# Attention and two expert layers on one core: an earlier load, a split moved to another engine, two small steps put later

## The chip, the cores and the metric

The kernel runs on one core of a Trainium2 chip. A core has a matrix engine (PE, with its weight loads shown as PEld), a vector engine (DVE), a scalar engine (ACT), a general engine (POOL), and a sync engine (SP) whose queue issues all DMA transfers of this kernel. The engines run beside each other, each one through its own instructions in a fixed order, and wait for each other by semaphores. The metric is the device time of one execution in microseconds (us); lower is better.

## What is computed

```
q, k, v: (2, 8, 576, 64)        1152 tokens, d_model 512
scores  = q @ k.T / 8
mask    = heads 0-3: 0 <= pos_q - pos_k < 32
          heads 4-7: pos_k <= pos_q and pos_q % 32 == pos_k % 32
x       = softmax(masked scores) @ v              -> (1152, 512)
p       = domain_probs / sum(domain_probs)        -> (1152, 4)
x2      = sum_e p[:, e] * (relu(x @ w1[e]) @ w2[e])    w1: (4, 512, 1024)
out     = (sigmoid(x2 @ wg) * (x2 @ wv)) @ wo          wg, wv: (512, 1536)
```

## The kernel before

**Attention.** Its 32 groups of scores (16 a batch: eight "strided" ones for heads 4 to 7, eight "local" ones for heads 0 to 3) pass through a pipeline that is written out by hand. At step i, `attention()` emits the scores and the exponentials of group i, the normalisation (`group_norm`) of group i-2, the transpose (`group_transpose`) of group i-4, the product with v of group i-5 and the copy into the token matrix (`group_split`) of group i-6. The first 23 steps (`FIRST_GROUPS`) run alone; the others are emitted between the first matmuls of the expert layer. `keep_warm` adds two matmuls with zeros to some steps.

In a step, DVE copies a transpose out of PSUM (L524), takes row maxima (L503), adds a small number to the row sums (L512) and inverts them (L513); POOL multiplies the probabilities by them (L514); for some steps DVE then rounds the result to its high part (L567, L561) and POOL subtracts to get the low part `xl` (L568, L562). ACT makes the exponentials (L505).

**Loads of q and k for the strided heads.** `load_strided_qk(b, c)` loads heads 4+2c and 5+2c of batch b, one DMA for q and one for k when b is 1, into a corner of the accumulator `x2acc` that is not in use yet (72 partitions x 2 x 512 floats, 295 KB each). `qk_strided` transposes them on PE (L445), in steps 13 and 15 for pair (1, 0) and in steps 17 and 18 for pair (1, 1). All loads stand in SP's queue in the order in which the program asks for them.

**Weights.** They come in 25 pieces of 512 x 512, in two raw loads each of 512 KB for the first 16, through three raw buffers. Pieces 0 to 3 are split into a high part (ACT, L425) and a low part (DVE, L427), both float32r, four chunks of 512 columns each. From step 14 on, `prep_some(0, 1)` does one such step behind each attention step, so that piece 0's four low parts follow steps 15, 17, 19 and 21. Pieces 4 to 15 are made half precision by `prep_half`: DVE takes maxima of both raw loads (L339) and of these (L344), PE spreads the maximum to all partitions (L251, in `scale_on_chip`), DVE makes a scale of it (L254 to L258), and ACT and DVE write the parts (L353, L355). `yield "hold"` ends the budget of the current tile; a tile is twelve matmuls (four triples L612, L613, L614), and each tile's end gives `prep_some` two or three steps.

**Token weights.** `token_weights()` is four small DVE operations (L194 to L197), `spread_token_weights()` a PE transpose (L201), a copy and two DMAs, which bring the first expert's weights to all partitions.

Of the kernel before, what the change touches and what calls it, by code (L numbers as in the profile page):

```python
# [9 lines left out]
F32 = mybir.dt.float32  # L10
# [7 lines left out]
ALU = mybir.AluOpType  # L18
# [15 lines left out]
FIRST_GROUPS = 23  # L34
# [4 lines left out]
def attn_moe_glu_kernel(ctx, tc, q, k, v, dp, w1, w2, wg, wv, wo, out):  # L39
    nc = tc.nc  # L40
# [206 lines left out]
    def scale_on_chip(col, m):  # L247

        ps = g_tile()
        top = m.bitcast(BF16)[:, 1:2]  # L250
        nc.tensor.matmul(ps[:, :128], top.to_broadcast([128, 128]), identb, start=True, stop=True)  # L251
        t = tmp["top"][:, n_top[0] % 2:n_top[0] % 2 + 1]
        n_top[0] += 1
        nc.vector.tensor_reduce(t, ps[:, :128], AX.X, ALU.max)  # L254
        nc.vector.tensor_scalar(t.bitcast(U32), t.bitcast(U32), 0x7F800000, None, ALU.bitwise_and)
        dn = tmp["down"][:, col:col + 1]
        nc.vector.tensor_scalar(dn, t, 2.0 ** -100, 1.0 / TOP, ALU.max, ALU.mult)
        nc.vector.reciprocal(tmp["up"][:, col:col + 1], dn)  # L258
        yield "hold"
# [69 lines left out]
    def w_pool(name):  # L329
        return tmp["w"] if name == "w2" else wp  # L330

    def prep_half(n):

        i, u, m = raw_list[n]
        r = held_raw[i, u] = raw.pop((i, u))
        if u == 0:
            held_raw[i] = tmp["p"].tile([128, 3], F32, tag="wpk", name="wpk")
        pk = held_raw[i]
        nc.vector.tensor_reduce(  # L339
            pk[:, u // 2:u // 2 + 1], r, AX.XY, ALU.max, apply_absolute_value=True)  # L340
        yield
        if u == 0:
            return
        nc.vector.tensor_reduce(pk[:, 2:3], pk[:, :2], AX.X, ALU.max)  # L344
        yield "hold"
        yield from scale_on_chip(i, pk[:, 2:3])
        (name, tag), = pool_of[i]
        t = w_pool(name).tile([128, 2, 4, 512], F16, tag=tag, name="w16")
        wh[i], wl[i] = t[:, 0], t[:, 1]
        sc = tmp["up"][:, i:i + 1]  # L350
        for c in range(4):
            part = held_raw[i, c // 2 * 2][:, c % 2, :]
            nc.scalar.activation(wh[i][:, c, :], part, AF.Copy, scale=sc)  # L353
            yield
            nc.vector.scalar_tensor_tensor(wl[i][:, c, :], part, sc, wh[i][:, c, :], ALU.mult, ALU.subtract)  # L355
            yield
            if c == 1:
                held_raw.pop((i, 0))
                load_raw_to(n + RAW_BUFS)
        for k_ in ((i, 2), i):  # L360
            held_raw.pop(k_)
        load_raw_to(n + 1 + RAW_BUFS)
# [48 lines left out]
    def prep_weights(n):  # L411
        i, u, m = raw_list[n]
        if i >= 2 * NST:
            yield from prep_gated(n)
            return
        if as_half(i // 2):
            yield from prep_half(n)
            return
        if u == 0:
            for d, (name, tag) in zip((wh, wl), pool_of[i]):  # L420
                d[i] = w_pool(name).tile([128, 4, 512], F32R, tag=tag, name=tag)
        r = raw.pop((i, u))
        hi_, lo_ = wh[i][:, u:u + m, :], wl[i][:, u:u + m, :]
        for x in range(m):
            nc.scalar.copy(hi_[:, x], r[:, x])  # L425
            yield
            nc.vector.tensor_tensor(lo_[:, x], r[:, x], hi_[:, x].bitcast(F32), ALU.subtract)  # L427
            yield
        load_raw_to(n + 1 + RAW_BUFS)

# [4 lines left out]
    def qk_strided(b, c, hhs):  # L435

        for hh in hhs:
            for nm, dst in (("qs", QT), ("ks", KT)):
                if hh == 0:
                    dst["s", b, c] = atp.tile([128, 2, 4, NU], F32, tag=nm + "T", name=nm + "T", bufs=2)  # L440
                src, t = qkv[nm, b, c], dst["s", b, c]
                ps = gp.tile([128, 512], F32, tag="g", name="qkps")
                pv_ = ps[:, :4 * NU].rearrange("p (a b) -> p a b", b=NU)
                for rp in range(4):
                    nc.tensor.transpose(  # L445
                        pv_[:, rp, :], src[:, hh, rp * 128:(rp + 1) * 128], ident[:NU, :NU]
                    )
                if nm == "qs":
                    nc.scalar.activation(t[:, hh], pv_, AF.Copy, scale=SCALE)
                else:  # L450
                    nc.vector.tensor_copy(t[:, hh], pv_)
        if hhs[-1] == 0:
            return
        if (b, c) == (0, 1):
            alloc_x(NT - 1)
        if (b, c) == (1, 0):
            load_strided_qk(1, 1)

    def qk_local(b, part):
        for nm, dst in (("ql", QT), ("kl", KT)):  # L460
# [142 lines left out]
    def g_tile():  # L603
        n_g[0] += 1
        pool = tmp["g"] if "g" in tmp and n_g[0] % 8 >= PSUM_BUFS else gp
        return pool.tile([128, 512], F32, tag="g", name="gps")
# [206 lines left out]
    with tc.manual_schedule():  # L813
        acc["x2"] = accp.tile([128, KC, NTOK], F32, tag="acc", name="x2acc")
        load_strided_qk(0, 0)
        load_strided_qk(0, 1)
        warm_up()
        make_constants()
        load_local(0)
        load_strided_v(0, 0)  # L820
        load_strided_v(0, 1)
        load_vl(0)
        nc.sync.dma_start(ptok, dp.rearrange("(t p) e -> p t e", p=128))
        for T in range(NT - 1):
            alloc_x(T)

        def attend():

            i = next(att, None)
            if i == 1:  # L830
                load_strided_qk(1, 0)
                load_raw_to(3)
            if i == 8:
                load_strided_v(1, 0)
            if i == 11:
                load_local(1)
            if i == 13:
                load_strided_v(1, 1)
            if i == 18:
                token_weights()  # L840
            if i == 19:
                spread_token_weights()
            if i == 20:
                load_vl(1)
            return i

        att = attention()
        for i in range(FIRST_GROUPS):
            attend()
            if i >= 14:  # L850
                prep_some(0, 1)
        n_none = 0
        halves = x_half()
        for n, u in enumerate(units):
            if u == ("u", EARLY, 0):
                for _ in halves:
                    pass
            if u[0] == "u" and u[1] == NST:
                while u[2] not in x2_done:
                    split_x2(1)  # L860
            if n == N_EARLY:
                while attend() is not None:
                    pass
                at_stack.close()
                tmp["p"] = ctx.enter_context(tc.tile_pool(name="tmp", bufs=2, side="right", reuse_waits="tile"))
                alloc_scales()
                late.append(raw_next[0])
                tmp["g"] = ctx.enter_context(
                    tc.tile_pool(name="gp2", bufs=8 - PSUM_BUFS, space=PSUM, side="right", reuse_waits="tile"))
                tmp["w"] = ctx.enter_context(tc.tile_pool(name="wp2", bufs=W_BUFS_2, side="right", reuse_waits="tile"))  # L870
            while any(i in pieces_of(u) for i in waiting()):
                prep_some(n, 1)
            if u == ("d", NST, 0):
                acc["out"] = accp.tile([128, NTB, DM], F32, tag="acc", name="outacc")
            if n >= N_EARLY:
                load_p_some(n)
                load_p_some(n)
            for y in unit_steps(u):
                if n < N_EARLY and y is None:
                    n_none += ATT_RATE  # L880
                    while n_none >= 1:
                        attend()
                        n_none -= 1
                if y == "evac":
                    if n >= N_EARLY:

                        if gated:
                            split_x2(2)
                            continue
                        if x16_next[0] < 2 or n > units.index(("u", EARLY - 1, x16_next[0] - 1)):  # L890
                            if next(halves, "end") != "end":
                                prep_some(n, 1)
                                continue
                    prep_some(n, 3 if u[1] >= NST else 2)
            if u[0] == "d" and u[1] == NST - 1:
                gated.append(x2_half(u[2]))
# [28 lines left out]
```

## Time and profile before

| | |
|---|---|
| median of 3 runs | 677.48 us (676.19 to 678.43) |
| profiled execution | 675.37 us, span 673.6 us |
| PE busy | 658.9 us, 98% of the span |
| DVE, ACT, POOL busy | 489.5, 269.0, 196.5 us |
| granted PE clock, mean | 0.992 of full speed |

The span is the profiled stretch from the first to the last instruction; 1.8 us of the execution's time lie around it. The profiled execution is 2.1 us below the median of the timed runs.

### The profile page before, as it was taken

How to read it: one execution, taken by the hardware profiler on the slowest of the kernel's cores; microseconds unless marked ns; L12 is line 12 of the kernel's file. 1: busy time of each engine (PE TensorE's matmuls, PEld its weight loads, DVE VectorE, ACT ScalarE, POOL GpSimd, SP SyncE). 2: the span in 40 equal slices, each digit the busy share in tenths (PEclk: the TensorE clock that was granted, in tenths of full speed). 3: DMA queues.
4: the chain of work that ended last, by engine and by line, in shares of the span. 5: the costliest groups of instructions: out<-in, count | busy, mean ns of one | idle time of the engine just before them, and what ended most of it. 6: DMA issues, size and time to landing. Idle time of an engine off the chain costs nothing.

```text
span 673.6 us, 11048 instructions
## 1 busy us (share of the span) xinstructions
PE 658.9 (98%) x4263; PEld 430.6 (64%) x4263; DVE 489.5 (73%) x986; ACT 269.0 (40%) x665; POOL 196.5 (29%) x218
## 2 busy tenths in 40 slices
PE   9979999999899999999999999999999999999998
PEld 5657899999766666666665656556655555555554
DVE  4866765888777777779798989887789898822212
ACT  6757631333344434442425252533355264331120
POOL 3634540000222222222345252522144244331110
PEclk9969999999999999999999999999999999999999
DMA  8944133011322342233221313111123321000002
GB/s 191 227 111 122 49 112 89 27 37 32 106 75 64 93 106 75 75 94 95 63 79 59 95 32 94 53 43 33 31 63 94 95 85 40 1 1 0 32 17 94
DMA packets 39029, 48.59 MB, mean 72 GB/s; under 512 B 18524, under 2 KB 23424, under 8 KB 38976
## 3 DMA queue, kind: packets, MB, share of 16 engines
q1 hardware_dynamic: 38976, 47.89, 25.0%
q8 instruction: 33, 0.54, 0.3%
q14 instruction: 20, 0.16, 0.1%
HBM read 45.50 MB, written 2.38 MB: 71 GB/s over the span
## 4 chain that ended last, share of the span: by engine, by line
PE 89%; DVE 8%; issue 1%; DMA 1%; ACT 1%; POOL 0%; SPq 0%; POOLq 0%; DVEq 0%; ACTq 0%
PE gps L612 27%; PE gps L613 27%; PE gps L614 27%; PE sps L495 2%; PE tps L521 1%; PE o L542 1%; PE warm L167 1%; DMA x2acc<-in_q_dram 1%; PE qkps L445 1%; DVE x2acc L676 1%; DVE wpk L339 1%; PE sps L485 1%; ACT P L505 1%; DVE x L290 1%; DVE magn L372 1%
## 5 line engine op out<-in xcount | busy, mean ns | idle before, releaser
L635 POOL TENSOR_TENSOR hl<-t,hh 128x384 f16<-128x384 f32 x72 | 69.3, 962 | 253.9 <-ACT t L634 249.8
L612 PEld LDWEIGHTS <-w 128*128 128x128 f16 x864 | 84.4, 98 | 56.2 <-issue 0.3
L614 PEld LDWEIGHTS <-w 128*128 128x128 f16 x864 | 84.4, 98 | 56.0
L613 PEld LDWEIGHTS <-w 128*128 128x128 f16 x864 | 84.4, 98 | 55.2
L633 ACT ACTIVATE hh<-gps 128x384 f16<-128x384 f32 x72 | 35.2, 489 | 148.3 <-PE gps L614 147.2
L612 PE MATMUL gps<-x,w 128*128 128x384 f16 x288 | 93.9, 326 | 0.0
L612 PE MATMUL gps<-hh,w 128*128 128x384 f16 x288 | 93.9, 326 | 0.0
L614 PE MATMUL gps<-x2p,w 128*128 128x384 f16 x288 | 93.9, 326 | 0.0
L614 PE MATMUL gps<-hh,w 128*128 128x384 f16 x288 | 93.9, 326 | 0.0
L613 PE MATMUL gps<-hl,w 128*128 128x384 f16 x288 | 93.9, 326 | 0.0
L613 PE MATMUL gps<-x,w 128*128 128x384 f16 x288 | 93.9, 326 | 0.0
L614 PE MATMUL gps<-x,w 128*128 128x384 f16 x288 | 93.9, 326 | 0.0
L613 PE MATMUL gps<-x2p,w 128*128 128x384 f16 x288 | 93.9, 326 | 0.0
L612 PE MATMUL gps<-x2p,w 128*128 128x384 f16 x288 | 93.9, 326 | 0.0
L699 POOL TENSOR_TENSOR hl<-gv,hh 128x384 f16<-128x384 f32 x36 | 34.7, 965 | 146.4 <-ACT hh L698 146.4
L355 DVE SCALAR_TENSOR_TENSOR w<-raw,up,w 128x512 f16<-128x512 f32 x48 | 38.4, 799 | 20.3 <-ACT w L353 20.3
L676 DVE TENSOR_TENSOR x2acc<-x2acc,t 128x384 f32<-128x384 f32 x84 | 49.7, 591 | 2.9
L673 DVE SCALAR_TENSOR_TENSOR t<-gps,comb,pb 128x384 f32<-128x384 f32 x72 | 43.9, 609 | 9.9 <-PE gps L614 9.9
L698 ACT CAST hh<-gv 128x384 f16<-128x384 f32 x36 | 18.4, 512 | 81.4 <-DVE gv L697 81.4
L697 DVE SCALAR_TENSOR_TENSOR gv<-gps,sg 128x384 f32<-128x384 f32 x36 | 20.0, 555 | 40.5 <-PE gps L614 40.3
L407 POOL TENSOR_TENSOR w<-magn,w 128x512 f16<-128x512 f32 x36 | 46.1, 1287 | 8.5 <-ACT magn L406 8.0
L353 ACT ACTIVATE w<-raw,up 128x512 f16<-128x512 f32 x48 | 33.0, 717 | 31.4 <-DVE up L258 31.0
(130 smaller groups left out, 1238.5 us busy)
## 6 DMA issues: line engine op xcount, KB each, us to landing
raw<-in_moe_w_dram SPq DMA_DIRECT2D x32, 512.0 KB
raw<-in_moe_w_gate_dram SPq DMA_DIRECT2D x12, 512.0 KB
raw<-in_moe_w_val_dram SPq DMA_DIRECT2D x12, 512.0 KB
raw<-in_moe_w_out_dram SPq DMA_DIRECT2D x12, 512.0 KB
pb<-pd SPq DMA_DIRECT2D x11, 192.0 KB
out_dram<-outacc SPq DMA_DIRECT2D x8, 256.0 KB
vl<-in_v_dram SPq DMA_DIRECT2D x8, 160.0 KB
vs<-in_v_dram SPq DMA_DIRECT2D x4, 288.0 KB
```

Of the source, the lines that this page charges most:

```text
L353: nc.scalar.activation(wh[i][:, c, :], part, AF.Copy, scale=sc)
L355: nc.vector.scalar_tensor_tensor(wl[i][:, c, :], part, sc, wh[i][:, c, :], ALU.mult, ALU.subtract)
L407: nc.gpsimd.tensor_tensor(wl[i][:, c, :], f, wh[i][:, c, :], ALU.subtract)
L612: nc.tensor.matmul(ps, ah, bh, start=i == 0, stop=False)
L613: nc.tensor.matmul(ps, ah, bl, start=False, stop=False)
L614: nc.tensor.matmul(ps, al, bh, start=False, stop=i == n - 1)
L633: nc.scalar.activation(dh, ps, AF.Relu, scale=DOWN)
L635: nc.gpsimd.tensor_tensor(dl, t, dh, ALU.subtract)
L673: nc.vector.scalar_tensor_tensor(t, ps, cc, pb[e, T], ALU.mult, ALU.mult)
L676: nc.vector.tensor_tensor(a, a, t, ALU.add)
L697: nc.vector.scalar_tensor_tensor(gv, pv_, DOWN, sg, ALU.mult, ALU.mult)
L699: nc.gpsimd.tensor_tensor(dl, gv, dh, ALU.subtract)
```

## The change

The load of pair (1, 1) is asked for behind step 1, next to pair (1, 0) and three raw loads, instead of at the end of step 15. Piece 0's four low parts are subtracted on POOL. The token weights are made and spread behind steps 23 and 24 instead of 18 and 19. In `prep_half` there is a second "hold" between the maximum of a piece and the matmul that spreads it.

```diff
@@ prep_half
         nc.vector.tensor_reduce(pk[:, 2:3], pk[:, :2], AX.X, ALU.max)
+        yield "hold"
         yield "hold"
         yield from scale_on_chip(i, pk[:, 2:3])
@@ prep_weights
             nc.scalar.copy(hi_[:, x], r[:, x])
             yield
-            nc.vector.tensor_tensor(lo_[:, x], r[:, x], hi_[:, x].bitcast(F32), ALU.subtract)
+            low = nc.gpsimd if i == 0 else nc.vector
+            low.tensor_tensor(lo_[:, x], r[:, x], hi_[:, x].bitcast(F32), ALU.subtract)
             yield
@@ qk_strided
-        if (b, c) == (1, 0):
-            load_strided_qk(1, 1)
@@ attend
             if i == 1:
                 load_strided_qk(1, 0)
                 load_raw_to(3)
+                load_strided_qk(1, 1)
...
-            if i == 18:
+            if i == FIRST_GROUPS:
                 token_weights()
-            if i == 19:
+            if i == FIRST_GROUPS + 1:
                 spread_token_weights()
```

On SP's queue, between steps 1 and 20, the order differs as follows (x2acc with q and k is the pair of the strided heads, vs and vl are v, ql and kl the local heads' q and k, raw the weights, pd and ptokT the token weights):

```order
 L143 DMA raw<-in_moe_w_dram 128x2x512 x3
+L82 DMA x2acc<-in_q_dram 72x2x512
+L82 DMA x2acc<-in_k_dram 72x2x512
 L90 DMA vs<-in_v_dram 72x2x512
 L101 DMA ql<-in_q_dram 128x9x64 x2
 L101 DMA kl<-in_k_dram 128x9x64 x2
 L90 DMA vs<-in_v_dram 72x2x512
-L82 DMA x2acc<-in_q_dram 72x2x512
-L82 DMA x2acc<-in_k_dram 72x2x512
```

The pair has moved ahead of both loads of vs and of the local heads' four loads.

On POOL, in steps 14 to 19 (P is the normalisation, xl the low part of a result, wl<-raw,wh the low part of a weight chunk):

```order
-L514 TENSOR_TENSOR P<-P,sm 96x384 x2
+L514 TENSOR_TENSOR P<-P,sm 96x384
+L429 TENSOR_TENSOR wl<-raw,wh 128x512
+L514 TENSOR_TENSOR P<-P,sm 96x384
 L568 TENSOR_TENSOR xl_167<-of,xh_166 128x288
 L514 TENSOR_TENSOR P<-P,sm 96x384
+L429 TENSOR_TENSOR wl<-raw,wh 128x512
 L514 TENSOR_TENSOR P<-P,sm 72x288
 L568 TENSOR_TENSOR xl_167<-of,xh_166 128x288
```

A subtraction of 512 columns now stands between two normalisations in every second step.

On DVE, where piece 6 is prepared (wpk its maxima, top the start of its scale), the rows were, in the kernel before:

```order
L339 TENSOR_REDUCE wpk<-raw 128x1
L675 TENSOR_TENSOR t<-gps,pb 128x384
L676 TENSOR_TENSOR x2acc<-x2acc,t 128x384
L339 TENSOR_REDUCE wpk<-raw 128x1
L344 TENSOR_REDUCE wpk<-wpk 128x1
L254 TENSOR_REDUCE top<-gps 128x1
```

and are, in the changed kernel:

```order
L676 TENSOR_TENSOR x2acc<-x2acc,t 128x384
L356 SCALAR_TENSOR_TENSOR w_2124<-raw,up,w_2124 128x512
L339 TENSOR_REDUCE wpk<-raw 128x1 x2
L344 TENSOR_REDUCE wpk<-wpk 128x1
L254 TENSOR_REDUCE top<-gps 128x1
L255 TENSOR_SCALAR top<-top 128x1
```

On PE, the matmul L251 that lies between L344 and L254 stood behind the first tile of its unit before, and stands behind the third now: 24 matmuls further down.

## Rows read from the trace of the kernel before

**Rows 1.** Page, part 1: busy us, share of the span, instructions.
```profile
PE 658.9 (98%) x4263; PEld 430.6 (64%) x4263; DVE 489.5 (73%) x986; ACT 269.0 (40%) x665; POOL 196.5 (29%) x218
```
**Rows 2.** PE's waits: us in total, times, longest.
```profile
PE qkps L445 <- DMA x2acc<-in_q_dram: 4.1, 1, 4.1
PE gps L251 <- DVE wpk L344: 2.0, 2, 1.7
...
PE gps L251 <- DVE gpk L396: 0.7, 1, 0.7
```
**Rows 3.** Windows around the longest wait: length, busy by engine, PEclk, DMA, GB/s.
```profile
36.40:38.40 2.00, 0.00 (x0) 0.00 (x0) 1.24 (x5) 2.00 (x12) 1.86 (x3) 0.95 0.79 205
38.40:40.50 2.10, 0.01 (x1) 0.04 (x1) 0.00 (x0) 1.10 (x8) 0.50 (x1) 0.50 0.65 158
40.50:48.50 8.00, 7.84 (x58) 5.82 (x59) 4.98 (x17) 3.21 (x15) 1.48 (x3) 0.50 0.21 66
```
**Rows 4.** Timeline of SP's queue: start, us to issue.
```profile
20.16 1.41 SPq L143 DMA_DIRECT2D raw<-in_moe_w_dram  x3
...
33.06 1.45 SPq L90 DMA_DIRECT2D vs<-in_v_dram  x1
34.55 0.45 SPq L82 DMA_DIRECT2D x2acc<-in_q_dram  x1
```
**Rows 5.** Chain of waits, the same stretch: start, us, what.
```profile
34.55 5.80 DMA x2acc<-in_q_dram
```
**Rows 6.** Windows ahead of the wait, columns as in rows 3.
```profile
20.00:28.00 8.00, 7.25 (x107) 5.09 (x103) 6.44 (x22) 5.65 (x29) 5.06 (x8) 1.00 0.95 281
28.00:32.00 4.00, 4.00 (x53) 3.12 (x49) 3.77 (x15) 3.11 (x15) 2.68 (x4) 1.00 1.08 166
```
**Rows 7.** Timeline of PE where the expert layer begins.
```profile
55.81 0.45 PE L613 MATMUL gps<-xl,wh 128*128 128x384 f32 x1 [0.53 <-POOL xl L568]
```
**Rows 8.** Subtractions on DVE and POOL: ns min/median/max; then by form, 26 to 57 us.
```profile
L427 DVE TENSOR_TENSOR wl<-raw,wh x16: 656/685/1276, 34.1 to 97.1; 128x512 fp32r<-128x512 f32 x16
...
L407 POOL TENSOR_TENSOR w<-magn,w x36: 1156/1304/1607, 333.1 to 592.4; 128x512 f16<-128x512 f32 x36
...
L568 POOL TENSOR_TENSOR xl<-of,xh 128x288 fp32r<-128x288 f32 x2 | 1.6, 790 | 0.0
...
L568 POOL TENSOR_TENSOR xl<-of,xh 128x96 fp32r<-128x96 f32 x2 | 0.8, 384 | 0.0
```
**Rows 9.** Timeline of DVE: small operations from SBUF to SBUF.
```profile
33.02 0.59 DVE L512 TENSOR_SCALAR sm<-sm 96x3 f32<-96x3 f32 x1
...
36.02 0.15 DVE L512 TENSOR_SCALAR sm<-sm 96x3 f32<-96x3 f32 x1
...
45.92 0.60 DVE L195 TENSOR_SCALAR psums<-psums 128x9 f32<-128x9 f32 x1
```
**Rows 10.** Timeline of POOL.
```profile
32.90 1.09 POOL L562 TENSOR_TENSOR xl<-of,xh 128x192 fp32r<-128x192 f32 x2
...
36.54 0.82 POOL L514 TENSOR_TENSOR P<-P,sm 96x384 f32<-96x384 f32 x1 [1.73 <-DVE sm L513]
...
45.70 0.79 POOL L568 TENSOR_TENSOR xl<-of,xh 128x288 fp32r<-128x288 f32 x1
...
54.75 0.66 POOL L514 TENSOR_TENSOR P<-P,sm 72x288 f32<-72x288 f32 x1 [1.74 <-DVE xh L567]
55.38 0.94 POOL L568 TENSOR_TENSOR xl<-of,xh 128x96 fp32r<-128x96 f32 x2
```
**Rows 11.** Timeline of DVE where piece 6's maximum is taken.
```profile
169.87 1.21 DVE L339 TENSOR_REDUCE wpk<-raw 128x1 f32<-128x1024 f32 x1
171.11 0.15 DVE L344 TENSOR_REDUCE wpk<-wpk 128x1 f32<-128x2 f32 x1
```
**Rows 12.** Timeline of PE, the last 24 matmuls ahead of the L251 that reads it.
```profile
165.51 0.34 PE L612 MATMUL gps<-x,w 128*128 128x384 f16 x1
...
169.26 0.33 PE L614 MATMUL gps<-x,w 128*128 128x384 f16 x1
```

## The prediction

> **What bounds the kernel now.** I read the page first: PE is busy for 658.9 of 673.6 us [rows 1], so no other engine's work counts unless PE waits for it or runs slower because of it. Next PE's own waits. Three matter: 4.1 us once for the DMA that brings q of a strided pair, 2.0 us in two waits for a weight piece's maximum (one of them 1.7), and 0.7 us for a later piece's [rows 2]. Then the windows around the long wait, where the reader is to see two losses, not one. PE does nothing from 36.4 to 40.5; from 38.4 on the granted clock is 0.50, that is 1.2 GHz, and it is still 0.50 in the eight microseconds after the wait, in which PE is busy for 7.84 [rows 3]. At 2.4 GHz that work takes about half, 3.9 us. So the late load costs up to 4.1 + 3.9 = 8.0 us.
>
> Why it is late: SP is in order, and it got to this load only at 34.55, behind a load of v that held it from 33.06 to 34.5 [rows 4]. From there it took 5.80 us to land, because the DMA engines were still busy with what was asked for earlier [rows 5, 6].
>
> Last, the place where attention hands over to the expert layer: PE's first matmul that needs the last low part `xl` of token block 0 starts at 55.81, after a wait for POOL [rows 7]. Whatever the change does in steps 14 to 22 shows as a shift of this one time; behind it PE is fed well enough that I carry the shift to the end.
>
> **The load, part by part.** In the new order the pair stands behind pair (1, 0) and three raw loads. These are 2 x 0.295 + 3 x 0.524 = 2.16 MB; the window from 20 to 28 us moved 281 GB/s x 8 us = 2.25 MB [rows 6], so the raws are in by about 28. The pair's 0.59 MB at the next window's 166 GB/s [rows 6] take 3.6 us: landed by 31.6. PE asks for it at 36.4 [rows 3]; the cover is nearly 5 us. The wait goes (gain 4.1) and with it the reason for the slow clock. Pair (1, 0) and the raws stand ahead of it and lose nothing. What is now behind it, two loads of v and the local q and k, lands up to 3.6 us later, but the same bytes are through by the same time as before, 34.55 + 5.80 = 40.35. The first of them to be used is local q and k, in step 21, which I put at about 44 below; if this cover went, PE would wait there instead.
>
> **What is late next.** Without the wait PE alone would come to the handover some 9 us earlier: 4.1 for the wait, 3.9 for the clock, and about 1.2 of small waits at 53 to 56. It won't, because POOL's row gets full. POOL's normalisation at 36.54 had 1.73 us of idle time before it [rows 10], into which the first low part fits. From there to the `xl` that PE needs, POOL now has: two normalisations of 384 columns (2 x 0.82), five of 288 (5 x 0.66), two `xl` of 288 columns (2 x 0.79), one split pair (0.94), the first of the last pair (0.38), and three low parts [rows 8, 10]. A low part on POOL is not in the trace. The nearest row is the subtraction of 512 columns with half-precision output, 1.16 to 1.61 us with a median of 1.30 [rows 8]; the same operation at 96 and 288 columns, 0.384 and 0.790, gives 2.1 ns a column and 1.26 us at 512. I take 1.29. The sum is 1.64 + 3.30 + 1.58 + 0.94 + 0.38 + 3.87 = 11.7, so POOL is done at 48.2 if it never waits. That makes 7.6 us instead of 9.
>
> It will wait. The operation L512 of DVE takes 0.15 us by itself but 0.59 at 33.02, where it began beside a POOL operation of 32.90 and ended with it; L195 did the same at 45.92, beside the POOL subtraction that began at 45.70 [rows 9, 10]. So a small DVE operation stands still until POOL's current one is through, and the next normalisation needs just this L512. Behind each of the three low parts, POOL then idles while DVE finishes L512, the reciprocal and a rounding: from L512's start at 36.02 to POOL's at 36.54 that is 0.5 us [rows 9, 10]. With a fourth, shorter one of 0.3 that is 1.8 us, and the handover is at 50.0: 5.8 us earlier. At two of the places DVE and POOL come within 0.1 us of each other by my count, and either could be first. I take 6.2 us, near the lower end of 5.8 to 7.6.
>
> The page "SBUF — State Buffer" of the Trainium skill, section "Who interferes with whom", says that such pairs hold a shared port as an exclusive lock, and that whoever comes first blocks the other for the whole instruction. By that rule the 5.8 stands and the 7.6 doesn't. The two long rows agree with it.
>
> What DVE is spared is the four low parts: 0.69 us each at the median, up to 1.28 beside POOL [rows 8]. I price this at nothing beyond the above, since POOL sets the pace there.
>
> **Token weights.** Four small DVE operations, the longest 0.60 us [rows 9], a short PE transpose, a copy and two DMAs go from steps 18 and 19 into the expert layer's first unit. PE pays for the transpose in either place. Their result is used by the first down unit, at least 14 triples later (42 matmuls at 0.163 = 6.8 us, worked out in the next part); the DMAs lie on a queue that is mostly idle by then (share 0.21 in rows 3). I price this at 0; if the two took as long as the late load, PE would wait up to 2 x 5.8 - 6.8 = 4.8 us. On SP the raw loads behind them move by as much, with two other raws in hand.
>
> **The second hold.** DVE is late for piece 6: its second maximum runs from 169.87 and L344 ends at 171.26, while PE was through at about 169.6 [rows 11, 12]. PE's matmul L251 now stands 24 matmuls further down. These take (169.26 - 165.51) / 23 = 0.163 us each [rows 12], 3.9 us together, against a wait of 1.7; DVE has one more L355 to do in between, under 0.8. So this wait goes, and the shorter one of piece 4, a tile further down, too: 2.0 us [rows 2]. The bounds are 0 and 2.0; nothing speaks for a part of it. Each of twelve pieces starts its scale a tile later, and the half-ready pieces of the last layer follow; counted in the program's order, pieces 20 and 23 are now written 6 tiles ahead of their first use instead of 13, 12 x 0.163 x 6 = 11.7 us. The 0.7 us of [rows 2] may come, go or double: plus or minus 0.7.
>
> **Sum.** 6.2 + 2.0 = 8.2. The profiled execution's 675.4 becomes 667.2. The median of the runs is 2.1 above it, so the prediction is 677.5 - 8.2 = 669.3.
>
> **The rivals.**
> *The clock falls again at the handover* (671 to 674). In the count above PE has its last work before the handover at about 48 and waits for `xl` until 50: 2 us, and before, the clock fell some 2.0 us after PE went idle [rows 3]. A second stretch of 10 us at 1.2 GHz, now under dense matmuls, costs 5 us: 674. Against it: if DVE wins either tie the gap is nearer 1 us.
> *POOL is worse than counted* (671 to 673). With low parts at 1.61 [rows 8] POOL needs 3 x 0.32 = 1.0 us more, and with an idle half microsecond in each of eight steps 2.2 more than the 1.8 taken: a gain of 6.2 - 3.2 + 2.0 = 5.0, 672.5. "GPSIMD Engine Reference" of the Trainium skill, section 3.1, speaks against this part of the change: it counts 2.6 cycles an element for a two-input operation there and keeps elementwise work on DVE; 512 elements at 1.2 GHz would be 1.11 us by its figure, an estimate. The rows agree on the ratio (1.30 against 0.69), and the outcome of the rule is this rival.
> *The wait only moves* (675 to 677.5). Local q and k land after step 21 asks for them. The wait and the slow clock of [rows 3] come back there, 8.0 us against the 6.2; what is left is the hold's 2.0. Against it: 40.35 is before 44 with 3.6 us to spare.
> *Slower* (above 679.5). The pieces that are now 6 tiles ahead are not in time: DVE would have to be 11.7 us behind in the last layer, and each microsecond beyond that is a microsecond of PE at pieces 20 and 23. It decides from 11.7 + 8.2 + 2 = 22 us on, 11 if both are late alike after the cover. Against it: nine L251 of that layer had one tile of cover, 2.0 us, and PE waited 0.7 in all [rows 2], so DVE was under 3 us behind.
>
> **Chances and range.** The forecast, 666 to 671: 0.65. Clock: 0.13. POOL: 0.12. The wait moved: 0.06. Slower: 0.03. Another 0.01 lies below. The likeliest is 669.3. The range goes down to 665.8 (7.6 for the handover, 2.0, and the 0.7 of the gpk waits, with about 1.4 from waits behind the handover that I didn't count) and up to 673.5, which takes in the POOL rival and most of the clock's. 0.3% of this kernel is 2.0 us, about what the measurement can tell from no change. Faster by more: 0.92; within: 0.05; slower: 0.03.
>
> **What would show it.** PE's wait for x2acc is gone, and the PEclk is 1.00 from 36 to 50: right on the load. PE's waits name POOL (L514, L568, L429) between 40 and 50 instead, and the first L613 that reads `xl` starts at 49.6, give or take 1: right on the next bound. The POOL rows of the low parts are 1.2 to 1.4 us, and L512 has rows of 0.5 us and more beside them. No wait of PE for L344. Wrong would be: a window with 0.50 behind the handover, PE waiting for ql or kl, or for a weight in the last layer.

## Result and the profile after

The changed kernel takes 669.87 us (median of 4 runs, 669.53 to 670.36) against 676.84 us (675.8 to 678.43, 4 runs) for the kernel before in the same comparison: a ratio of 0.9896, 95% interval 0.9873 to 0.9918. The profiled execution has a span of 668.3 us instead of 673.6. Two executions further down, of 845.45 us (u_load) and 1746.33 us (hold_some, its first profiled one), are out of line with all others and stand in no median or ratio.

The page of the changed kernel, part 1, and the line of the granted clock in 40 slices (9 is 90% or more of full speed; the third slice, which holds the wait, was a 6 before):

```profile
PE 655.2 (98%) x4258; PEld 429.0 (64%) x4263; DVE 483.3 (72%) x982; ACT 267.9 (40%) x665; POOL 200.4 (30%) x222
...
PEclk9999999999999999999999999999999999999999
```

PE's waits in the changed kernel, in the columns of [rows 2]:

```profile
PE gps L251 <- DVE gpk L397: 3.4, 2, 1.7
PE tps L521 <- POOL P L514: 2.0, 5, 0.9
...
PE gps L613 <- POOL xl L568: 0.6, 1, 0.6
```

The wait for x2acc and the waits for the half-precision pieces (wpk) are gone, 6.1 us together. POOL's normalisations stand in the first one's place with 2.0 us, as the prediction had it. The top row has grown: 3.4 us for two pieces of the last layer, where it was 0.7 for one.

The same stretches as in [rows 3], and the one up to the handover:

```profile
36.40:38.40 2.00, 1.06 (x13) 0.92 (x12) 1.93 (x8) 1.79 (x9) 1.60 (x3) 1.00 1.06 232
38.40:40.50 2.10, 2.10 (x39) 1.70 (x37) 1.65 (x4) 1.72 (x11) 2.10 (x3) 1.00 0.83 188
40.50:48.50 8.00, 6.96 (x84) 5.11 (x82) 7.34 (x22) 7.42 (x41) 6.79 (x10) 1.00 0.62 149
48.50:50.10 1.60, 0.81 (x5) 0.24 (x3) 1.06 (x5) 1.60 (x8) 1.20 (x4) 1.00 0.53 116
```

The clock is 1.00 where it was 0.50, and DVE, ACT and POOL are all nearly full: where one transfer held the stretch up, three engines are now near their limit in it.

SP's queue of the changed kernel, as in [rows 4]:

```profile
21.41 0.48 SPq L82 DMA_DIRECT2D x2acc<-in_q_dram  x1
21.93 0.39 SPq L82 DMA_DIRECT2D x2acc<-in_k_dram  x1
...
30.20 6.34 SPq L101 DMA_DIRECT2D kl<-in_k_dram  x2
36.63 1.01 SPq L90 DMA_DIRECT2D vs<-in_v_dram  x1
```

The load is asked for 13.1 us earlier. The second load of v is now last, 3.6 us later than before, and nothing waits for it.

The handover on PE, as in [rows 7], then POOL and DVE where the second low part stands (their timelines):

```profile
50.09 0.44 PE L613 MATMUL gps<-xl,wh 128*128 128x384 f32 x1 [0.64 <-POOL xl L568]
```

```profile
39.42 1.28 POOL L429 TENSOR_TENSOR wl<-raw,wh 128x512 fp32r<-128x512 f32 x1
41.10 0.66 POOL L514 TENSOR_TENSOR P<-P,sm 72x288 f32<-72x288 f32 x1 [0.40 <-PE tps L521]
```

```profile
39.77 0.95 DVE L512 TENSOR_SCALAR sm<-sm 72x4 f32<-72x4 f32 x1
40.76 0.17 DVE L513 RECIPROCAL sm<-sm 72x4 f32<-72x4 f32 x1
```

Read the three together: L512 begins 0.35 us after POOL's subtraction and ends when that one does (40.70); the reciprocal and a rounding follow; POOL starts its next normalisation 0.40 us after it became free. The profile puts this wait of POOL down to a transpose. But POOL has five such gaps from 36 to 50 us, put down to four different operations, and in all five it starts 0.17 or 0.18 us after the reciprocal's end; so what it waits for is DVE. Without POOL beside it L512 would have been done at about 39.9 (0.15 us alone), well before POOL was free.

### The profile page after: what moved, and what is told of

It is laid out like the page before. It is cut to its first block, busy times and chain, and to the rows that moved or that the text cites. A ratio compares the mean times of both kernels' runs of the same rounds, so it can differ in the third digit from the quotient of the medians.

```text
span 668.3 us, 11027 instructions
## 1 busy us (share of the span) xinstructions
PE 655.2 (98%) x4258; PEld 429.0 (64%) x4263; DVE 483.3 (72%) x982; ACT 267.9 (40%) x665; POOL 200.4 (30%) x222
## 4 chain that ended last, share of the span: by engine, by line
PE 85%; DVE 10%; ACT 2%; issue 1%; POOL 1%; ACTq 0%; POOLq 0%; DVEq 0%
PE gps L612 26%; PE gps L613 26%; PE gps L614 26%; PE sps L495 2%; PE tps L521 2%; DVE bits L377 1%; DVE magn L380 1%; PE warm L167 1%; PE o L542 1%; DVE bits L375 1%; DVE x2acc L676 1%; DVE bits L371 1%; DVE outacc L725 1%; DVE gpk L393 1%; ACT magn L407 1%
## 5 line engine op out<-in xcount | busy, mean ns | idle before, releaser
L676 DVE TENSOR_TENSOR x2acc<-x2acc,t 128x384 f32<-128x384 f32 x84 | 51.8, 617 | 2.9
L408 POOL TENSOR_TENSOR w<-magn,w 128x512 f16<-128x512 f32 x36 | 44.4, 1232 | 25.6 <-ACT magn L407 24.7
L254 DVE TENSOR_REDUCE top<-gps 128x1 f32<-128x128 f32 x27 | 7.9, 291 | 51.4 <-PE gps L251 51.3
L505 ACT ACTIVATE P<-sps,nm 72x72 f32<-72x72 f32 (+1 forms) x112 | 36.4, 334 | 16.5 <-DVE sm L512 12.4
```

Source lines behind the costliest of these rows:

```text
L408: nc.gpsimd.tensor_tensor(wl[i][:, c, :], f, wh[i][:, c, :], ALU.subtract)
L505: nc.scalar.activation(pp[:, j, :], pv_[:, j, :], AF.Exp, bias=nm[:n, j:j + 1], accum_out=sm[:n, j:j + 1])
L676: nc.vector.tensor_tensor(a, a, t, ALU.add)
```

## Experiments

Each kernel is the changed one or the one before with the edit shown. "Handover" is the start of the first matmul that reads the last `xl` (55.81 before, 50.09 after), from the profile of each; ratios are to the kernel before, timed beside each group, with 95% intervals. An edit shifts the line numbers behind it: the reciprocal is L513 in the changed kernel and L512 in no_add, the normalisation L514 and L513.

| kernel | handover, us | median, us | ratio (interval) |
|---|---|---|---|
| changed kernel | 50.09 | 669.87 | 0.9896 (0.9873 to 0.9918) |
| u_load | 58.33 | 678.09 | 1.0019 (1.0005 to 1.0032) |
| u_hold | 49.48 | 669.25 | 0.9888 (0.987 to 0.9906) |
| u_low | 49.73 | 669.41 | 0.9886 (0.9867 to 0.9904) |
| u_tok | 53.49 | 672.08 | 0.9928 (0.9906 to 0.995) |
| load_only | 49.50 | 669.17 | 0.989 (0.9875 to 0.9906) |
| load_tok | 49.83 | 669.08 | 0.988 (0.9866 to 0.9893) |
| hold_only | 55.78 | 677.0 | 0.9997 (0.998 to 1.0015) |
| no_add | 47.43 | 666.6 | 0.9847 (0.9833 to 0.986) |
| low_dve | 47.90 | 667.28 | 0.9866 (0.985 to 0.9881) |
| hold_some | 46.71 (second profile) | 663.75 | 0.9814 (0.98 to 0.9828) |
| hold_both | 47.91 | 664.33 | 0.9823 (0.9809 to 0.9836) |

**u_load: the load back to step 15, all else as changed.**

```diff
-                load_strided_qk(1, 1)
...
+        if (b, c) == (1, 0):
+            load_strided_qk(1, 1)
```

> The changed kernel with the load of pair (1, 1) put back to the end of step 15. Theory (the late load costs a wait of 4 us and some 8 to 10 us at 1.2 GHz): PE waits about 4 us for x2acc again, the clock is 0.50 behind it, the handover's first L613 on xl is back at 55 to 56.5 instead of 50.1, and the time is 5 to 7 us above the changed kernel (675 to 677). Rival (POOL and DVE would be the bound of these steps anyway): the handover moves by 2 us or less.

PE's longest wait and the window behind it in this kernel:

```profile
PE qkps L447 <- DMA x2acc<-in_q_dram: 6.0, 1, 6.0
```

```profile
42.00:50.60 8.60, 7.30 (x54) 5.39 (x54) 2.99 (x9) 2.82 (x12) 1.41 (x2) 0.50 0.25 65
```

The theory holds, and by more than it said: the wait is 6.0 us here instead of 4, the clock is 0.50 up to 50.6, the handover comes 8.2 us later, and all of the gain is gone. The other three edits by themselves win nothing; the interval (1.0005 to 1.0032) speaks for a small loss.

**load_only: the load alone, in the kernel before.**

```diff
-        if (b, c) == (1, 0):
-            load_strided_qk(1, 1)
...
                 load_raw_to(3)
+                load_strided_qk(1, 1)
```

> The kernel before with the early load alone. Theory (the load brings all of the gain, the other edits trade): PE's wait for x2acc is gone, the handover is at 50 to 53, and the time is 5 to 7 us below the kernel before; the clock may still fall in some executions, as it did with the token weights in steps 18 and 19. Rival (the gain needs the move of the low parts too): 3 us below or less.

669.17 us, the time of the whole change, and 8.0 us below the kernel before where 5 to 7 were expected. The rival is out: the move of the low parts isn't needed for it.

**u_hold and hold_only: the second hold.** The first takes it out of the changed kernel (shown), the second puts it alone into the kernel before.

```diff
         nc.vector.tensor_reduce(pk[:, 2:3], pk[:, :2], AX.X, ALU.max)
-        yield "hold"
         yield "hold"
```

> The changed kernel with a single hold in prep_half. Theory from the trace after (the second hold removes 2.0 us of waits for the half-precision pieces and moves the last pieces to places where PE waits 3.4 us instead of 0.7 for gpk): the wait of 1.7 for L344 is back near 165, the gpk waits fall to about 0.7, and the time is 0.5 to 1 us below the changed kernel. Rival, the prediction's own step (only the gain of 2.0 hangs on the hold): 2 us above it.

> The kernel before with the second hold alone. Theory (waits for wpk of 2.0 us go, those for gpk rise from 0.7 to 3.4): 0 to 1 us above the kernel before. Rival, the prediction's step: 2 us below.

PE's waits without the hold, then with the hold alone:

```profile
PE gps L251 <- DVE wpk L344: 2.0, 2, 1.7
...
PE gps L251 <- DVE gpk L396: 0.7, 1, 0.7
```

```profile
PE gps L251 <- DVE gpk L397: 3.3, 2, 1.7
PE qkps L446 <- DMA x2acc<-in_q_dram: 3.0, 1, 3.0
```

Both show the trade: 2.0 us of one wait for 2.6 more of the other. The times agree with it (0.6 below the changed kernel; 0.9997 of the kernel before), though 0.6 us is less than the intervals can tell. The prediction's 2 us is out.

Where the 3.3 comes from: the chain of waits in the changed kernel ahead of one of the two.

```profile
568.24 0.60 DVE gpk L393
568.84 0.02 issue
568.87 0.17 DVE gpk L397
569.03 0.05 issue
569.08 0.24 PE gps L251
```

In the program's order this piece's maximum now falls in the third tile of an up unit (a layer's first matrix product), right behind a down unit (its second); in the kernel before it fell in the seventh. DVE was busy for 7.86 of the 8 us before 565, with the accumulation of that down unit between the steps of the preparation, and one tile of cover isn't enough for its lag there. The place alone doesn't do it: five of the layer's nine pieces now stand there, and PE waits for the last two. Only they have this accumulation (L725) ahead of them, three times 0.74 us each; its first one in the program starts at 559.0:

```profile
L725 DVE SCALAR_TENSOR_TENSOR outacc<-gps,cv,outacc x19: 483/750/752, 559.0 to 664.7; 128x512 f32<-128x512 f32 x17, 128x256 f32<-128x256 f32 x2
```

**u_low: the low parts back on DVE.**

```diff
-            low = nc.gpsimd if i == 0 else nc.vector
+            low = nc.vector
```

> The changed kernel with all low parts on DVE. Theory A (DVE is given four subtractions of 0.7 to 1.3 us but no longer stands still for POOL's 1.27 us ones, about 0.8 us four times): the handover is within 1 us of 50.1 and the time within 1 us. Theory B (the subtractions on DVE were the bound that the move took away): the handover is 2 us or more later and the time 2 us or more above the changed kernel.

Theory A holds: the handover is 0.36 us earlier, and the time can't be told from the changed kernel's. The operation L512 between 33 and 50 us, min/median/max in ns, in the changed kernel and in this one:

```profile
L512 DVE TENSOR_SCALAR sm<-sm x8: 242/698/1252, 33.7 to 47.7; 72x4 f32<-72x4 f32 x5, 96x3 f32<-96x3 f32 x3
```

```profile
L512 DVE TENSOR_SCALAR sm<-sm x8: 150/156/600, 34.1 to 48.1; 72x4 f32<-72x4 f32 x5, 96x3 f32<-96x3 f32 x3
```

Moving 0.7 to 1.3 us of work from DVE to POOL made a 0.16 us operation of DVE take 0.70 at the median. What DVE was given back it spent standing still.

**u_tok and load_tok: the token weights.**

```diff
-            if i == FIRST_GROUPS:
+            if i == 18:
...
-            if i == FIRST_GROUPS + 1:
+            if i == 19:
```

> The changed kernel with the token weights behind steps 18 and 19 again. Theory (POOL and DVE in turn set the pace of these steps, so 1.2 us of DVE work there counts in full or nearly): the handover is 0.5 to 1.5 us later and the time as much above. Rival (priced at nothing in the prediction): within 0.3 us.

> The kernel before with the early load and the later token weights, without the second hold and with all low parts on DVE. Theory (these two edits are what gains; the other two together cost 0.5 to 1 us): 668.2 to 669.0, at or below the changed kernel, clock 1.00 throughout, waits for wpk of 2.0 and for gpk of 0.7. Rival (the two others gain when both are there): 670 or more.

With the low parts on POOL (u_tok) the early token weights cost 2.2 us at the median, and 3.4 at the handover of the profiled execution, where 0.5 to 1.5 were expected; PE waits for them, and then the clock falls:

```profile
PE pps L201 <- DVE ptok L197: 1.0, 1, 1.0
```

```profile
41.00:44.00 3.00, 1.49 (x14) 0.76 (x11) 2.86 (x10) 1.87 (x9) 1.60 (x3) 1.00 0.51 150
44.10:50.90 6.80, 6.80 (x54) 5.08 (x53) 4.16 (x16) 5.14 (x27) 5.33 (x7) 0.50 0.50 117
```

PE was busy for half of the three microseconds ahead, in short pieces with no gap above 1.03 us, and ran the next 6.8 us at half the clock. The runs of u_tok lie in two clusters, and the mean granted clock that the record has for each run tells them apart: 1.000 in the three of 670.4 to 671.1, 0.995 in the three of 673.1 to 673.5. So the old place costs 0.5 to 1.2 us, as the theory had it, and some 2.7 more in the executions in which the clock falls.

With the low parts on DVE (load_only against load_tok, which is load_only with the token weights late) their place makes no difference, 669.17 against 669.08, although PE waits for them in load_only too:

```profile
PE pps L201 <- DVE ptok L197: 1.1, 1, 1.1
```

The mean clock of load_only is 0.999 or 1.000 in each run, so this wait by itself doesn't bring it down. What brings it down in half of the runs of u_tok was not found.

**no_add: without L512.** It leaves out the addition of 1e-9 to the row sums.

```diff
-        nc.vector.tensor_scalar(sm, sm, 1e-9, None, ALU.add)
```

> The changed kernel without L512, the addition of 1e-9 to the row sums, which are at least 1; so this leaves out the one small DVE operation that stood still beside POOL's subtractions. Theory (it is this standstill that puts the handover at 50.1 rather than at 48.2): DVE's idle or blocked time in steps 16 to 22 goes, POOL's low parts are followed by the next normalisation without the 0.4 us of idle time, the handover comes 1 to 1.8 us earlier and the time falls by as much. Rival (the reciprocal or the rounding of xh will stand still in its place): handover and time within 0.5 us.

POOL and DVE around the second low part in this kernel:

```profile
38.23 1.26 POOL L429 TENSOR_TENSOR wl<-raw,wh 128x512 fp32r<-128x512 f32 x1
39.46 0.72 POOL L513 TENSOR_TENSOR P<-P,sm 72x288 f32<-72x288 f32 x1
...
44.50 0.66 POOL L513 TENSOR_TENSOR P<-P,sm 72x288 f32<-72x288 f32 x1
```

```profile
38.56 0.16 DVE L512 RECIPROCAL sm<-sm 72x4 f32<-72x4 f32 x1
38.65 1.01 DVE L566 CAST xh<-of 128x288 fp32r<-128x288 f32 x1
```

The reciprocal is not held up, POOL goes from one operation to the next without a gap, and 3.3 us are won, 2.7 of them at the handover; the theory had 1 to 1.8. The rival is right that the rounding stands still in L512's place (1.01 us instead of 0.28), but no normalisation waits for it. POOL is 0.83 us earlier before the first low part already (33.82 against 34.65, the normalisation ahead of it), as L512 was held up by other POOL work there too; between that and the last `xl` it saves 1.9. The idle time there was five times 0.40, of which the prediction had four at 1.8 together.

**low_dve: as no_add, with the low parts on DVE and a single hold.**

> The changed kernel without L512, with all low parts on DVE and a single hold. Theory (without L512 DVE no longer stands still for POOL, and with the low parts it has 3 to 4 us more to do in steps 15 to 21, beside POOL operations that slow them): the handover is 0.5 to 1.5 us later than the 47.4 of the kernel without L512; time 666 to 667.5, as the single hold gives back 0.6. Rival (DVE has room for them, and ACT is the bound of these steps): the handover at 47.4 or earlier, 666 or less.

The handover is 0.47 us later than in no_add, and the time 0.7 us above it, with the hold's difference in it. Once L512 no longer couples the two engines, the move to POOL costs nothing and may be worth half a microsecond; the intervals overlap.

Against load_tok this kernel differs by L512 alone, and it is 1.9 us ahead at the handover (47.90 against 49.83) with no low part on POOL in either. So no_add's gain isn't all standstill beside the low parts: L512's own time on a full DVE (busy for 15.15 of the 16 us from 32 to 48 in load_tok), and its standstill beside other POOL work, are in it. What bounds these steps next was not tested; ACT is busy for 15.59 of the 16 us from 32 to 48 here, and for 15.51 in no_add.

**hold_some and hold_both: no_add with the hold where it helps.** hold_some has the second hold for pieces 4 to 7 only (shown); hold_both has one for the last layer's pieces as well.

```diff
-        yield "hold"
+        if i < 8:
+            yield "hold"
         yield "hold"
```

> The changed kernel without L512 (the 1e-9 is left out) and with the second hold for pieces 4 to 7 only. Theory (the second hold gains where DVE is late for pieces 4 and 6, and loses only because eight further tiles of delay move pieces 23 and 24 to the third tile of an up unit): no wait for wpk, gpk waits of 0.7 or less, since the pieces' maxima fall in the first tile of a down unit now; 2.5 to 3.5 us below the kernel without L512, 663 to 664. Rival (the places of the late pieces matter little, and some other one waits): within 1 us of 666.6.

> As the one before, and with a second hold for the last layer's pieces too. Theory (a tile more between maximum and matmul covers DVE's lag wherever the pieces fall): no wait for gpk either, though the pieces' maxima fall in up units again; within 1 us of the one before. Rival (the lag in an up unit is more than two tiles): gpk waits of 1 us or more.

> The same kernel as hold_some, for a profile of an undisturbed execution. Theory: no wait of PE for wpk, gpk waits of 0.7 us or less, a wait for x2pk of 1.5 at the most; span 661 to 663, of which the handover is 47.4 to 48.

The second profile of hold_some (hold_some_look) comes with the times 662.89 and 663.1 and a ratio of 0.9794 (0.975 to 0.9839). PE's longest wait in it, and in hold_both:

```profile
PE gps L251 <- DVE gpk L398: 1.0, 1, 1.0
```

```profile
PE gps L251 <- DVE x2pk L315: 1.3, 1, 1.3
```

The waits for wpk are gone in both, and of the 3.3 us for gpk 1.0 and nothing are left; the theory's 0.7 was a little low, and its handover (47.4 to 48) late. The two kernels are the same within their intervals. hold_some has the lowest time here, by the ratios 12 to 14 us below the kernel before and 5 to 7 below the changed one.

## Why the prediction was right, point by point

**Right: the load.** The wait of 4.1 us and the half clock behind it are both gone; u_load and load_only show from both sides that this edit makes the gain. The rival in which the wait only moves didn't come: nothing waited for local q and k.

**Right: the next bound, and its size.** The sum over POOL's operations with the standstill gave 50.0 for the handover, and it came at 50.09; L429 took 1.272 us on average where 1.29 was taken. That it fits to 0.1 us is luck: the normalisation from which the sum starts came at 37.10 and not at 36.54, because the first low part did not fit into the idle time without a standstill (L512 took 1.25 us beside it), while POOL's operations took 11.3 us instead of 11.7 and its four gaps 1.6 instead of 1.8. I took 6.2 us instead of the 5.8 that this gave, in view of two ties that DVE might win; it won none, and the profile shows 5.7. One reading was loose: at 33.02 L512 ended with the first of the two POOL operations of the row at 32.90, at 33.6, and not with the row, at 33.99; the standstill is the same. That L512 holds the handover up was shown by no_add; that it is by the standstill is read from the rows, and low_dve shows that it is not all of it.

The page "SBUF — State Buffer" of the Trainium skill, section "Who interferes with whom", agrees with these rows: whichever of the two engines comes second waits for the whole instruction. Here that is DVE; the other way round is in load_tok, where a normalisation of 288 columns that POOL began at 43.12, beside DVE's subtraction of 42.98 to 43.67, took 1.08 us instead of 0.66.

**Wrong: the second hold, 2.0 us.** The wait for wpk went as forecast, but the step "the 0.7 us of [rows 2] may come, go or double: plus or minus 0.7" failed. It became 3.4. The twelve holds moved the last layer's pieces by 7 to 11 tiles (one by 22), the last two into a place where DVE lags behind by more than a tile; I had weighed only whether the pieces would be ready for their first use, not where their maxima would stand. In PE's waits the term is 2.0 won against 2.7 lost, -0.7 instead of +2.0; the times put it between 0 and -0.6, within their intervals.

**Half right: the low parts.** "I price this at nothing" holds for the sum (u_low, within 0.5 us), but the cover I named, that POOL sets the pace, was made by the move: without it POOL is busy for 10.71 of the 16 us from 34 to 50 instead of 13.99, and the handover comes as late all the same. DVE (14.51) and ACT (14.69) are nearly full there; that L512's going brings the handover 1.9 us forward without the move (low_dve) speaks for DVE, but which of them sets the pace was not settled.

**Missed: the token weights.** Priced at 0, which is true with the low parts on DVE. With them on POOL they would cost 2.2 us at the median in their old place, so putting them later pays for a cost that the move of the low parts makes. The clock rival, which the prediction put at the handover, did not come there: where the rival had PE idle for 2 us, PE was busy for 1.21 of the last 2.0. It showed at the old place of the token weights instead.

**The sum.** In the two profiled executions the handover gives 5.7 and the rest, 617.8 us before and 618.2 after, nothing: 5.3 of span against the 8.2 predicted. In the medians it is 7.0. The kernel before varies by 2.1 to 5.5 us in each comparison (674.1 to 679.6 over all), the changed one by 0.8, and the record's clock of each run shows a reason. In the 44 executions of the kernel before beside the experiments, the eleven with a mean granted clock of 0.992, as in the profiled one, took 676.0 us on average, the seven with 0.987 took 678.5; the changed kernel has 0.999 or 1.000 in all four. So the half-clock stretch varies from one execution to the next, and the profile that the costs were read from had one of the shorter ones. hold_only, with a shorter wait for the load (3.0 us), has the longer stretch: 0.63 of the clock from 36 to 42 and 0.50 up to 51, where the kernel before was back at 1.00 by 48.5. That this makes up all of the 1.7 us between profiles and medians was not shown. So that 669.3 came out at 669.87 is in part luck: the hold's missing 2.7 us were made up for the most part by these 1.7, probably because the late load costs more in most executions than in the quick one I read it from.

## What to carry to other kernels

Where PE waits for a load, count the slow clock behind the wait as well as the wait, and then look for the engine that is full next; the gain ends there, not at PE's own pace. Before moving work from DVE to POOL, look for the smallest DVE operation that stands between two POOL operations: if it lengthens beside POOL, the move may buy nothing while it is there, as here. A delay put into a chain of preparation steps shifts everything behind it, so check where each later step falls, and put it only on the pieces that need it.

## What the runs showed of the hardware

A DVE addition on 72 x 4 or 96 x 3 numbers took 0.15 us alone and up to 0.96 and 1.25 beside a POOL subtraction, while the reciprocal on the same numbers took 0.16 or 0.17 in either case, and a rounding of 288 columns went from 0.28 to 1.01 (no_add). The granted clock fell to half not only after an idle PE (before, 4.1 us of waiting) but also behind three microseconds in which PE was half busy in short pieces (u_tok); just before the changed kernel's handover, with PE busy for 0.81 of 1.60 us, it stayed at 1.00. It fell in some executions of one kernel and not in others: three of six for u_tok. SP's issue of two loads of the local heads took 6.3 us (30.20 in the changed kernel) while the DMA share was 0.91.
